# A rational FFN behind masked attention: splitting three blocks of results with one cast and one subtraction, one wide place for the parts and four places for V

## Chip, cores and metric

The kernel runs on one core of one Trainium2 chip. The metric is the time of one launch on the device, in microseconds (us), as the median of several runs. The names used below are PE for TensorE (matmul; PEld is its weight load), DVE for VectorE, ACT for ScalarE, POOL for GpSimd and SP for SyncE.

## The reference

Attention over 8 batches of 8 heads with 576 positions and 64 columns each keeps only scores within `tau` of a row's maximum. Its output, 4608 rows of 512 columns, goes through a feed-forward layer whose activation is a ratio of two polynomials:

```python
scores = scale * np.matmul(q, k.transpose(0, 1, 3, 2))
thresh = np.max(scores, axis=-1, keepdims=True) - tau
scores = np.where(scores >= thresh, scores, -1000000000.0)
attn = np.exp(scores - np.max(scores, axis=-1, keepdims=True))
attn = attn / (np.sum(attn, axis=-1, keepdims=True) + 1e-09)
attn_out = np.matmul(attn, v)
x = attn_out.transpose(0, 2, 1, 3).reshape(B * S, H * D)
h = x @ w_in                      # 512 -> 2048
P = a[0] + a[1] * h + a[2] * h**2 + a[3] * h**3
Q = 1.0 + np.abs(b[0]) * np.abs(h) + np.abs(b[1]) * h**2
g = P / (Q + 1e-06)
return g @ w_out                  # 2048 -> 512
```

## The kernel before

**Attention.** Heads go in pairs; a batch has four pairs. A unit is one tile of 128 query rows of a pair, or the remainder of 64 rows. PE computes the scores of both heads (L812 and L816, the remainder L805) into banks of PSUM. DVE takes the negated maxima (L822), ACT applies the threshold (L837) and the exponential with its sum (L841). DVE and ACT scale the result and split it into a high and a low half of 16 bits (L326 or L328, then L863). A transposing DMA on SP's queue brings both into `pT`, and PE multiplies them with V, which is split in the same way (L934), into a chunk `x` of 256 rows for the second part. In the first batch the transposition is done by PE (L886, L891) and the product in 32 bits (L917).

**V's places.** V of a pair is loaded (L691) into one of `NV` places. A place comes free when the last product of its pair is done. The scale of a batch's V is found from the maxima of all four pairs (L431 is PE's step in it), so the first product of a batch needs all four to be loaded. The loads stand on POOL's queue from the third batch on, with those of Q and K.

**Feed-forward.** A group is four blocks of 128 of the 2048 columns, for one chunk of 256 rows; there are 72 groups, and the last one is done as two halves. The first product (L1051) is 48 matmuls. ACT brings it to SBUF with a scale (L1060), 1024 columns wide. Then come: the absolute value (L1065 on ACT or L1067 on DVE), two steps of the polynomials on DVE (L1071, L1074), a third (L1084), logarithm and exponential on ACT (L1078, L1081) for the reciprocal, and three more steps on DVE (L1087, L1090, L1093), the last of which gives the results `r`. The first of a group's four blocks goes into the second product as it is, in 32 bits (L1114). The other three are split in parts: a cast (`f_gh`, on ACT at L318 or on DVE at L320) rounds a block of 256 columns to the format `fp32r`, and a subtraction on DVE (`f_gl`, L1101) leaves what the rounding lost. PE multiplies the parts with the two parts of the weights, three matmuls for each block and half of the rows (L1110). The parts of one block lie in a place `g`, of which there are two; a place is free when the six matmuls that read it are done.

**Who sets the order.** Nothing is ordered by hand. The class `Plan` knows a duration for each operation, what it waits for and which places it takes and gives back. It lays out all operations in time on all engines, and the instructions are then written in that order. Operations in the table `FLEX` may go to ACT or DVE; the planner picks one by weighing the two with the factors `START`, `EARLY` and `PRICE`, each in its own stretch of time (`sooner`). Where PE would be idle near the start, it is given filler matmuls (L1254). A place of a pool is taken by the operation that comes next in its line. So a change of a duration or of a pool moves instructions on every engine.

Of the kernel before, what the change touches and what calls it, by code (L numbers as in the profile page):

```python
# [8 lines left out]
F32 = mybir.dt.float32  # L9
F32R = mybir.dt.float32r  # L10
F16 = mybir.dt.float16
# [4 lines left out]
ALU = mybir.AluOpType  # L16
# [7 lines left out]

POOLS = {"e": 3, "hi": 2, "pT": 2, "st": 8, "sc": 2, "t": 8, "u": 3, "g": 2, "x": 3, "xr": 1}

B2, B3, BA, B1, BH = [(0, 1, 2), (3, 4, 5)], [(0, 1, 2)], [(3,), (4,), (5,)], [(7,), (6,), (5,)], [(5,), (6,)]


LEAD, SPACE0, SPACING = 4.776489494, 2.7365, 2.085146464
ENDK, ENDS = 4.7452, 10.130284218

WHEN = [(-4.7413, 1.6268), (5.5534, 0.8332), (13.0267, 0.2709), (15.0744, 0.5122)]

V0, V1 = -3.870384768, -4.680004432

SINGLE = 21

VISITED = 8

FIRST = [(0, 0, 8), (1, 0, 16), (0, 8, 16)]
LAST = (0, 1, 2)
SOON = 1

NQ = 2

NV = 5

EARLY_BP = 8

# [4 lines left out]
PARTS = 3  # L57
# [2 lines left out]

ALL = 2.0 ** 100

PLAIN = (0, 1, 2, 3, 4)

UP = 2.0 ** -14
TPD = 1.3
# [11 lines left out]
        "ev": {"ACT": 0.465, "DVE": 0.6}, "ev1": {"ACT": 0.156, "DVE": 0.196}, "A": {"ACT": 0.583, "DVE": 0.341},  # L78
        "gh": {"ACT": 0.31, "DVE": 0.2}, "wh": {"ACT": 0.57, "DVE": 0.38}, "vc": {"ACT": 0.7, "DVE": 0.25}, "twice": {"ACT": 0.2, "DVE": 0.13}}

START = {"ACT": 2.958800008, "DVE": 3.4788}
START_END = 61.53014116
EARLY = {"ACT": 2.0183, "DVE": 2.9268}
EARLY_END = 1205.239479456
PRICE = {"ACT": 0.7389, "DVE": 2.6699}

TOL = {"PE": 0.098890645, "ACT": 0.1137, "DVE": 0.0398, "POOL": 0.1, "DMA": 0, "GD": 0}
WARM, WARM_END = 0.6, 400.0

LOADS_END = 120.0  # L90

LATE = 2.0

SPARE = {'t': 2, 'u': 1, 'g': 1, 'sc': 1}

# [24 lines left out]
class Plan:  # L120
# [21 lines left out]
    def op(self, eng, dur, key, fn, after=(), take=(), drop=()):  # L142
        engs = {eng: dur} if isinstance(eng, str) else eng
        o = Op(engs, key, fn, [x for x in after if x is not None], list(take), list(drop))
        o.rank, o.tiling = self.rank, "ff"
        self.ops.append(o)
        return o
# [10 lines left out]
    def sooner(self, e, t, o, free, can):  # L158
        price = START if t < START_END else EARLY if t < EARLY_END else PRICE
        for x, dur in o.engs.items():  # L160
            if x != e:
                begin = max(free[x], o.ready[x])
                begin += sum(p.engs[x] for p in can[x] if p.key < o.key and len(p.engs) == 1 and p.ready[x] <= begin)
                if begin + dur * price[x] < t + o.engs[e] * price[e]:
                    return True
        return False

    def order(self):
# [6 lines left out]
        free = dict.fromkeys(engines, 0.0)  # L175
        tiling = "f"
# [13 lines left out]
        while left:  # L190
            best = None
            for e in engines:
                starts = []
                for o in can[e]:
                    t = max(free[e], o.ready[e])
                    for h in o.take:
                        spot = None if h.pool in line and line[h.pool][-1] is not h and len(self.pools.get(h.pool, ())) <= SPARE.get(h.pool, 99) else self.spot(h, t)
                        if spot is None:
                            t = None
                            break  # L200
                        t = max(t, spot[0])
                    if t is not None:
                        if e == "PE":
                            t = max(t, free[e] + TURN.get((tiling, o.tiling[0]), 0.0))
                        starts.append((t, o))
                if not starts:
                    continue
                first = min(t for t, _ in starts)
                starts = sorted([x for x in starts if x[0] <= first + TOL[e]] if all(len(o.engs) == 1 for _, o in starts)
                                else starts, key=lambda x: (x[1].key, x[1].n))  # L210

                keep = [(t, o) for t, o in starts if len(o.engs) == 1 or not self.sooner(e, t, o, free, can)]
                if not keep:
                    continue
                first = min(t for t, _ in keep)
                t, o = min(((t, o) for t, o in keep if t <= first + TOL[e]), key=lambda x: (x[1].key, x[1].n))
                if best is None or t < best[0]:
                    best = (t, o, e)
            assert best is not None, "no op can start"
            t, o, e = best  # L220
# [3 lines left out]
            if e == "PE" and self.warm is not None and t < WARM_END:  # L224
                n = int((t - free[e]) * WARM / 0.22)
# [10 lines left out]
            if e == "PE":  # L236
                tiling = o.tiling[1]
# [34 lines left out]
def fr(ap):  # L272
    return ap.bitcast(F32R)
# [3 lines left out]
def masked_attention_rational_ffn(  # L277
# [12 lines left out]
    nc = tc.nc  # L290
    B, NP, D, S = qT.shape
    S = S // 2
    DM, DFF = w_in.shape
    P = 128
    NT = S // P
    REM = S - NT * P
    NF = DFF // P
    NFP = NF // 2
    NC = DM // P
    CT = 256  # L300
# [4 lines left out]
    op = plan.op  # L305
# [10 lines left out]
    def copy(dst, src):  # L316
        if plan.eng == "ACT":
            nc.scalar.copy(dst, src)  # L318
        elif plan.eng == "DVE":
            nc.vector.tensor_copy(dst, src)  # L320
        else:
            nc.gpsimd.tensor_scalar(dst, src, 1.0, 1.0, ALU.mult, ALU.mult)
# [9 lines left out]
    def tensor_tensor(dst, x, y, how):  # L332
# [5 lines left out]

    forms = {"t": ([P, 4 * CT], F32), "u": ([P, DM], F32), "e": ([P, 2 * S], F32), "hi": ([P, 2 * S], F16),
             "pT": ([P, 2, 2, 2 * NT + 1, P], F16), "st": ([P, 8], F32), "sc": ([P, 4], F32),  # L340
             "g": ([P, 2, CT], F32), "x": ([P, 2, NP, CT], F16), "xr": ([P, 2, NP, CT], F16)}
    places = {x: [const.tile(f, d, name=f"{x}{i}") for i in range(POOLS[x])] for x, (f, d) in forms.items()}

    def place(h):
        return places[h.pool][h.slot]
# [181 lines left out]
    for i in range(NW):  # L527
        pieces = []
        for c in range(NC):
            n = i * NC + c  # L530
# [6 lines left out]
            key = w_key(i, c)  # L537

            o6, box = decode_ops(n, key, load, hold)
# [9 lines left out]
        key = w_key(i, NC)  # L549
# [17 lines left out]
    wo_done = []  # L567

    def in_parts(f):
        return f % NC >= NC - PARTS  # L570

    for f in range(NF):
# [6 lines left out]
        key = w_key(f // NC, NC + f % NC)  # L579
# [5 lines left out]
        o, box = decode_ops(NC * NW + f, key, load, hold)  # L585
# [15 lines left out]
    visits = []  # L601
    for bb in range(B):
        v0 = bb * NP
        if bb < VISITED:
            visits += [(v0 + i, half) for i in range(NP - 1)] + [(v0 + NP - 1, half + other + rest)]
            visits += [(v0 + i, other + rest) for i in range(NP - 2, -1, -1)]
        else:
            visits += [(v0 + i, half + other + rest) for i in range(NP)]
# [60 lines left out]

    def is_plain(bp, t):  # L670

        return bp < NP and t in PLAIN

    v_ops = {}

# [343 lines left out]
    def moe_ops(ck, f0, nb, p, begins, ends, soon):  # L1019
# [18 lines left out]
        def on(e, d, *rest):  # L1038
            return op(e, size(e, d), *rest)
# [52 lines left out]
        def f_g():  # L1092
            nc.vector.scalar_tensor_tensor(box["r"], box["r"], a0, box["q"], ALU.add, ALU.mult)  # L1093

        def f_gh(j):
            box["g", j] = place(hg[j])
            copy(fr(box["g", j][:, 0]), box["r"][:, j * CT:(j + 1) * CT])

        def f_gl(j):
            g = box["g", j]  # L1100
            nc.vector.tensor_tensor(fr(g[:, 1]), box["r"][:, j * CT:(j + 1) * CT], g[:, 0], ALU.subtract)  # L1101

        def f_g2(j, tt):
            f = f0 + j
            if begins and j == 0:
                acc[tt] = bank(ah[tt])
            if in_parts(f):
                g = box["g", j][:, :, tt * P:(tt + 1) * P]
                for n, (x, y) in enumerate(((0, 0), (1, 0), (0, 1))):
                    nc.tensor.matmul(acc[tt], fr(g[:, x]), fr(wo[f][y]), start=begins and j == n == 0,  # L1110
                                     stop=ends and j == nb - 1 and n == 2)
                return
            o = j * CT + tt * P
            nc.tensor.matmul(acc[tt], box["r"][:, o:o + P], wo[f], start=begins and j == 0, stop=ends and j == nb - 1)  # L1114
# [30 lines left out]
                                       wi_done[g] + x_done[ck] + wo_done[f0:f0 + nb] + last_g1 if prev is None else [prev],  # L1145
                                       [bhs[j // 2]] if (j % 2, part) == (0, 0) else (), [xo, xo])
        last_g1[:] = [prev]
        hh, hq, hr = Hold("t", 1), Hold("t", 1), Hold("t", 2 * nb)
        n = 1 if kind == "m" else 4
        hs = [b for b in ([bb] if kind == "m" else range(4 * bb, 4 * bb + 4))]  # L1150
        h = None
# [8 lines left out]
        r3 = on("DVE", 0.638, p + 0.67, f_r3, [r2])  # L1160
        ln = on("ACT", 0.632, p + 0.7, f_ln, [q, r3])
        iv = on("ACT", 0.563, p + 0.75, f_inv, [ln])
        e = on("DVE", 0.6075, p + 0.85, f_e, [iv])
        nn = on("DVE", 0.6075, p + 0.9, f_n, [e], (), [hh])
        gd = on("DVE", 0.638, p + 0.95, f_g, [nn, r3], (), [hq])
        hg, gl = {}, {}
        for j in range(nb):
            if in_parts(f0 + j):
                hg[j] = Hold("g", 2)
                o = op(FLEX["gh"], 0, p + 0.97, lambda j=j: f_gh(j), [gd], [hg[j]], [hr])  # L1170
                gl[j] = op("DVE", 0.335, p + 0.98, lambda j=j: f_gl(j), [o], (), [hr])
        if begins:
            accs[ck] = {}, [Hold("acc", 1, BA) for _ in range(2)]
        acc, ah = accs[ck]
# [3 lines left out]
            each.sort(key=lambda x: x[1])  # L1178
        for i, (j, tt) in enumerate(each):
            starts = begins and j == 0  # L1180
            o = op("PE", 0.705 if j in hg else 0.859, p + 1.7 + 0.1 * i, lambda j=j, tt=tt: f_g2(j, tt),
                   [gl.get(j, gd), wo_done[f0 + j], prev, None if starts else last_g2.get(tt)],
                   [ah[tt]] if starts else (), [hg.get(j, hr)])
            prev = last_g2[tt] = o
        if ends:
            prev = None
# [42 lines left out]
    for bb in range(1, B - 1):  # L1229
        order += [(("m", bb, c), range(0, NF, NC)) for c in range(2)]  # L1230
        if bb % 4 == 3:
            order.append((("r", bb // 4, 0), range(0, NF, NC)))
    p = 0.0
    for ck, fs in order:
        kind, bb, c = ck
# [61 lines left out]
```

## Time and profile before

| what | value |
|---|---|
| median of three runs | 1279.27 us (1278.4 to 1280.01) |
| time of the profiled execution | 1281.68 us |
| span of the profiled execution, first to last instruction | 1279.9 us |
| mean granted clock of TensorE | 0.994 |
| busy: PE, DVE, ACT, POOL | 1246.4, 1199.3, 1074.5, 231.3 us |
| first product, L1051, 3072 records with chunks `x` | 374.7 us |
| split second product, L1110, 1296 | 355.2 us |
| subtractions, L1101, 216 on DVE | 86.6 us |
| casts of results, 123 on ACT and 93 on DVE | 47.8 and 25.7 us |

A busy time is the time in which at least one instruction of the group ran; the mean of one is its own duration. On a full engine the durations of neighbours overlap, so the pitch from one to the next is shorter than the mean. A 32-bit matmul of the program (not of `fp32r`) leaves two records. In the tables by stretches of time, the columns are the stretch, its length, the busy time of PE, PEld, DVE, ACT and POOL with the number of instructions, then the granted clock, the share of the DMA engines and GB/s; where one line of the code is asked for, only the engine in question stands there. In the waits, the columns are the engine with what it was to do, what it waited for, the total in us, the number of times and the longest. In the groups, busy time and mean in ns are followed by the idle time just ahead of them and what ended it.

### The profile page before, as it was taken

The page shows a single profiled execution, that of the slowest core. Times are in us where ns is not written, and L with a number is a line of the kernel's source. Part 1 is how long each engine was busy: PE and PEld are TensorE (multiplying, and loading weights), DVE is VectorE, ACT ScalarE, POOL GpSimd, SP SyncE. Part 2 cuts the span into 40 slices and gives each one's busy share as a digit, 9 for nine tenths or more (in the row PEclk, how much of TensorE's full clock was granted, in tenths as well). Part 3 has the DMA queues.
Part 4 walks back from the last instruction along what each step waited for, and adds up shares of the span by engine and source line. Part 5 has one row for each costly group of instructions (what it writes and reads, how often), then busy time and mean ns, then how long its engine had stood idle before and what let it go on. Part 6 is the DMA issues. An engine that isn't in the chain of part 4 may idle for free.

```text
span 1279.9 us, 25127 instructions
## 1 busy us (share of the span) xinstructions
PE 1246.4 (97%) x9252; PEld 889.8 (70%) x9252; DVE 1199.3 (94%) x1960; ACT 1074.5 (84%) x2180; POOL 231.3 (18%) x480
## 2 busy tenths in 40 slices
PE   8899999999999999999999999999999999999998
PEld 6576676676767667766667667677776667677775
DVE  5899999999999999999999899999999999997876
ACT  5999888989999888888897699999988998874454
POOL 2112000132132311332022140322121221100000
PEclk9999999999999999999999999999999999999999
DMA  7645246688667656776442765876566665530000
GB/s 216 174 143 163 78 105 112 134 144 154 105 133 132 146 107 119 142 137 126 91 105 56 131 141 111 142 135 136 104 120 125 130 123 112 111 71 17 18 17 17
DMA packets 338251, 146.64 MB, mean 115 GB/s; under 512 B 314416, under 2 KB 320720, under 8 KB 338128
## 3 DMA queue, kind: packets, MB, share of 16 engines
q1 hardware_dynamic: 316528, 87.67, 38.5%
q0 software_dynamic: 21280, 56.78, 16.4%
q8 instruction: 73, 1.20, 0.4%
q10 hardware_dynamic: 320, 0.59, 0.2%
q14 instruction: 50, 0.41, 0.1%
HBM read 60.30 MB, written 9.44 MB: 54 GB/s over the span
## 4 chain that ended last, share of the span: by engine, by line
PE 53%; DVE 27%; ACT 8%; issue 5%; DMA 3%; SPq 0%; DVEq 0%; ACTq 0%
PE banks L1051 16%; PE banks L1110 15%; PE banks L1114 6%; PE banks L934 6%; PE banks L816 5%; DVE e L863 4%; DVE st L822 3%; DMA pT<-e 2%; DVE t L1071 2%; DVE t L1087 2%; DVE t L1090 2%; PE banks L805 2%; DVE t L1084 2%; DVE t L1093 2%; DVE g L1101 2%
## 5 line engine op out<-in xcount | busy, mean ns | idle before, releaser
L1051 PEld LDWEIGHTS <-wi 128*128 128x128 f16 x3456 | 324.1, 98 | 144.1 <-issue 108.0
L1051 PE MATMUL banks<-x,wi 128*128 128x256 f16 x3072 | 374.7, 275 | 3.0 <-ACT t L1060 1.7
L1110 PE MATMUL banks<-wp,g 128*128 128x512 f32 x1296 | 355.2, 415 | 1.9 <-ACT g L318 1.2
L1110 PEld LDWEIGHTS banks<-wp,g 128*128 128x128 f32 x1296 | 234.0, 189 | 70.9 <-issue 15.5
L837 ACT ACTIVATE e<-banks,st 128x576 f32<-128x576 f32 x288 | 206.4, 735 | 18.5 <-DVE st L831 11.1
L841 ACT ACTIVATE e<-e,cf 128x576 f32<-128x576 f32 x288 | 221.0, 774 | 0.3
L863 DVE SCALAR_TENSOR_TENSOR e<-e,st,hi 128x576 f16<-128x576 f32 x252 | 203.5, 808 | 3.9 <-ACT hi L326 3.4
L822 DVE TENSOR_REDUCE st<-banks 128x2 f32<-128x1152 f32 x128 | 171.8, 1342 | 12.9 <-PE banks L816 10.8
L326 ACT ACTIVATE hi<-e,st 128x576 f16<-128x576 f32 x177 | 134.0, 769 | 51.9 <-DVE st L852 41.1
L816 PE MATMUL banks<-KK,QQ 64*128 64x512 f32 x512 | 144.5, 641 | 0.0
L1114 PE MATMUL banks<-wp,t 128*128 128x512 f32 x288 | 142.2, 608 | 1.7 <-DVE t L1093 1.6
L1060 ACT ACTIVATE t<-banks,hsc 128x512 f32<-128x512 f32 (+1 forms) x192 | 106.3, 575 | 25.9 <-PE banks L1051 24.7
L934 PEld LDWEIGHTS <-V 128*64 128x64 f16 x2520 | 104.1, 111 | 33.8 <-issue 32.6
L934 PE MATMUL banks<-pT,V 128*64 128x256 f16 (+1 forms) x2520 | 118.9, 249 | 3.0 <-DMA pT<-e 3.0
L1087 DVE SCALAR_TENSOR_TENSOR t<-t,co,t 128x1024 f32<-128x1024 f32 (+1 forms) x73 | 92.0, 1261 | 22.7 <-ACT t L1081 22.7
L1078 ACT ACTIVATE t<-t,co 128x1024 f32<-128x1024 f32 (+1 forms) x73 | 82.7, 1133 | 12.8 <-DVE t L1084 12.7
L1093 DVE SCALAR_TENSOR_TENSOR t<-t,co,t 128x1024 f32<-128x1024 f32 (+1 forms) x73 | 92.0, 1261 | 0.5
L1071 DVE SCALAR_TENSOR_TENSOR t<-t,co 128x1024 f32<-128x1024 f32 (+1 forms) x73 | 92.0, 1260 | 0.0
L1084 DVE SCALAR_TENSOR_TENSOR t<-t,co,t 128x1024 f32<-128x1024 f32 (+1 forms) x73 | 91.9, 1260 | 0.0
L1074 DVE SCALAR_TENSOR_TENSOR t<-t,co 128x1024 f32<-128x1024 f32 (+1 forms) x73 | 91.9, 1259 | 0.0
L1101 DVE TENSOR_TENSOR g<-t,g 128x256 fp32r<-128x256 f32 x216 | 86.6, 414 | 2.0 <-ACT g L318 1.6
L1090 DVE SCALAR_TENSOR_TENSOR t<-t,t 128x1024 f32<-128x1024 f32 (+1 forms) x73 | 87.7, 1201 | 0.4
(137 smaller groups left out, 1518.2 us busy)
## 6 DMA issues: line engine op xcount, KB each, us to landing
KK<-in_kT_dram POOLq DMA_DIRECT2D x84, 144.0 KB, 3.9
t<-in_w_in_dram POOLq DMA_DIRECT2D x16, 512.0 KB, 5.8
t<-in_w_out_dram POOLq DMA_DIRECT2D x16, 512.0 KB, 4.7
V<-in_v_dram POOLq DMA_DIRECT2D x24, 256.0 KB, 4.4
out_dram<-u POOLq DMA_DIRECT2D x24, 256.0 KB, 2.7
QQ<-in_qT_dram POOLq DMA_DIRECT2D x42, 144.0 KB, 3.1
QQ<-in_qT_dram POOLq DMA_DIRECT2D x42, 128.0 KB, 3.4
KK<-in_kT_dram SPq DMA_DIRECT2D x24, 144.0 KB, 3.5
```

The costliest lines, as they stand in the source:

```text
L326: nc.scalar.activation(dst, src, AF.Identity, scale=factor)
L816: nc.tensor.matmul(d, QQ[r, t * P:(t + 1) * P], KK[r, REM:S], **one)
L822: nc.vector.tensor_reduce(box["st"][:, 0:2], box["both"], AX.X, ALU.max, negate=True)
L837: nc.scalar.activation(ev(hh), box["s"][hh], AF.Prelu, scale=SCALE, bias=box["st"][:, 2 + hh:3 + hh], alpha=STEEP)
L841: nc.scalar.activation(e, e, AF.Exp, scale=passes, accum_out=box["st"][:, 4 + hh:5 + hh])
L863: nc.vector.scalar_tensor_tensor(box["lo"][:, c], ev(hh), box["st"][:, 6 + hh:7 + hh], box["hi"][:, c], ALU.mult, ALU.subtract)
L934: nc.tensor.matmul(dst, V[:, c * P + head * D:c * P + (head + 1) * D], rhs, start=c == 0 and n == 0, stop=c == NT and n == 2)
L1051: nc.tensor.matmul(d, wi_tile(c, f0 + j, hl), x[:, c, :], start=c == 0 and n == 0, stop=c == NC - 1 and n == 2)
L1071: nc.vector.scalar_tensor_tensor(box["r"], box["h"], a2, box["h"], ALU.add, ALU.mult)
L1087: nc.vector.scalar_tensor_tensor(box["q"], box["q"], qc, box["i"], ALU.add, ALU.mult)
L1110: nc.tensor.matmul(acc[tt], fr(g[:, x]), fr(wo[f][y]), start=begins and j == n == 0, stop=ends and j == nb - 1 and n == 2)
L1114: nc.tensor.matmul(acc[tt], box["r"][:, o:o + P], wo[f], start=begins and j == 0, stop=ends and j == nb - 1)
```

## The change

The cast and the subtraction of a group's blocks in parts become one instruction each, over the columns of all these blocks: 768 for a whole group, 256 and 512 for the two halves of the last one. Their place `g` is three times as wide, and there is one instead of two. V has four places instead of five. The planner's durations for the two operations follow, the planner looks at places when it weighs an engine (`sooner`), and a number of its factors have other values. Names that are new beside these (`REST_FIRST`, `STICK`, the form of `PLAIN`, the last lines on `LAST`) have values with which they change nothing by themselves.

```diff
-POOLS = {"e": 3, "hi": 2, "pT": 2, "st": 8, "sc": 2, "t": 8, "u": 3, "g": 2, "x": 3, "xr": 1}
+POOLS = {"e": 3, "hi": 2, "pT": 2, "st": 8, "sc": 2, "t": 8, "u": 3, "g": 1, "x": 3, "xr": 1}
...
-LEAD, SPACE0, SPACING = 4.776489494, 2.7365, 2.085146464
-ENDK, ENDS = 4.7452, 10.130284218
+LEAD, SPACE0, SPACING = 4.46212747, 2.7365, 2.085146464
+ENDK, ENDS = 4.7452, 7.461352888
...
-NV = 5
+NV = 4
...
-EARLY_END = 1205.239479456
-PRICE = {"ACT": 0.7389, "DVE": 2.6699}
+EARLY_END = 1196.621762778
+PRICE = {"ACT": 0.779887252, "DVE": 2.581335568}
...
-                begin = max(free[x], o.ready[x])
+                begin = max([free[x], o.ready[x]] + [self.spot(h, 0.0)[0] for h in o.take])
...
-             "g": ([P, 2, CT], F32), "x": ([P, 2, NP, CT], F16), "xr": ([P, 2, NP, CT], F16)}
+             "g": ([P, 2, PARTS * CT], F32), "x": ([P, 2, NP, CT], F16), "xr": ([P, 2, NP, CT], F16)}
...
-        def f_gh(j):
-            box["g", j] = place(hg[j])
-            copy(fr(box["g", j][:, 0]), box["r"][:, j * CT:(j + 1) * CT])
-
-        def f_gl(j):
-            g = box["g", j]
-            nc.vector.tensor_tensor(fr(g[:, 1]), box["r"][:, j * CT:(j + 1) * CT], g[:, 0], ALU.subtract)
+        split = [j for j in range(nb) if in_parts(f0 + j)]
+        GW = len(split) * CT
+
+        def f_gh():
+            box["g"] = place(hg)[:, :, 0:GW]
+            copy(fr(box["g"][:, 0]), box["r"][:, split[0] * CT:split[0] * CT + GW])
+
+        def f_gl():
+            g = box["g"]
+            nc.vector.tensor_tensor(fr(g[:, 1]), box["r"][:, split[0] * CT:split[0] * CT + GW], g[:, 0], ALU.subtract)
...
-                g = box["g", j][:, :, tt * P:(tt + 1) * P]
+                o = (j - split[0]) * CT + tt * P
+                g = box["g"][:, :, o:o + P]
...
-        hh, hq, hr = Hold("t", 1), Hold("t", 1), Hold("t", 2 * nb)
+        hh, hq, hr = Hold("t", 1), Hold("t", 1), Hold("t", 2 * (nb - len(split) + 1))
...
-        hg, gl = {}, {}
-        for j in range(nb):
-            if in_parts(f0 + j):
-                hg[j] = Hold("g", 2)
-                o = op(FLEX["gh"], 0, p + 0.97, lambda j=j: f_gh(j), [gd], [hg[j]], [hr])
-                gl[j] = op("DVE", 0.335, p + 0.98, lambda j=j: f_gl(j), [o], (), [hr])
+        n = len(split)
+        hg = Hold("g", 2 * n)
+        gh = {e: d * n + (n - 1) * -{"ACT": 0.098, "DVE": 0.07}[e] for e, d in FLEX["gh"].items() if e == "DVE" or not soon}
+        gh = op(gh, 0, p + 0.97, f_gh, [gd], [hg], [hr])
+        gl = op("DVE", 0.068 + 0.2667 * n, p + 0.98, f_gl, [gh], (), [hr])
```

Three places show how the instructions move. The first is DVE in the middle of the program, at the split of the 26th group: `t5_73` holds its results, `g0_96` and `g1_97` are the two places, `e0_79`, `st0_86` and `hi1_83` belong to the softmax and `V2_163` is a place of V. Before:

```order
L1101 TENSOR_TENSOR g1_97<-t5_73,g1_97 128x256
L863 SCALAR_TENSOR_TENSOR e0_79<-e0_79,st0_86,hi1_83 128x576
L950 SCALAR_TENSOR_TENSOR xr0_101<-banks_67,xr0_101 128x64
L863 SCALAR_TENSOR_TENSOR e0_79<-e0_79,st0_86,hi1_83 128x576
L1101 TENSOR_TENSOR g0_96<-t5_73,g0_96 128x256
L750 SCALAR_TENSOR_TENSOR V2_163<-V2_163,sx_166,u0_76 128x640
L320 CAST g1_97<-t5_73 128x256
L320 COPY V2_163<-u0_76 128x640
L1101 TENSOR_TENSOR g1_97<-t5_73,g1_97 128x256
```

The same engine at the split of the 26th group after the change (`t2_70` holds the results; L1101 is now the last step of the polynomials and L1112 the subtraction):

```order
L1101 SCALAR_TENSOR_TENSOR t2_70<-t2_70,co_126,t4_72 128x1024
L325 CAST g0_96<-t2_70 128x768
L1075 TENSOR_SCALAR t5_73<-t7_75 128x1024
L1112 TENSOR_TENSOR g0_96<-t2_70,g0_96 128x768
L1079 SCALAR_TENSOR_TENSOR t1_69<-t7_75,co_126 128x1024
L1082 SCALAR_TENSOR_TENSOR t5_73<-t5_73,co_126 128x1024
```

The cast and subtraction of the group stand together right behind its results, instead of three pairs spread among the softmax's instructions. Over the whole program DVE has 216 subtractions before and 73 after, 93 casts before and 35 after; ACT has 123 casts before and 38 after.

The second place is PE at the end of the program, where the last whole group ends (`wp11` is its last block's weights) and the two halves follow (blocks 12 and 13, then 14 and 15). Before:

```order
L1110 MATMUL banks_67<-wp11_1_153,g0_96 128x512
L1114 MATMUL banks_67<-wp12_154,t3_71 128x512 x2
L1110 MATMUL banks_67<-wp13_0_155,g1_97 128x512 x2
L1110 MATMUL banks_67<-wp13_1_156,g1_97 128x512
L1110 MATMUL banks_67<-wp13_0_155,g1_97 128x512 x2
L1110 MATMUL banks_67<-wp13_1_156,g1_97 128x512
L1110 MATMUL banks_67<-wp14_0_157,g0_96 128x512 x2
L1110 MATMUL banks_67<-wp14_1_158,g0_96 128x512
L1110 MATMUL banks_67<-wp15_0_159,g1_97 128x512 x2
```

After:

```order
L1122 MATMUL banks_67<-wp11_1_152,g0_96 128x512
L1126 MATMUL banks_67<-wp12_153,t2_70 128x512 x2
L1122 MATMUL banks_67<-wp13_0_154,g0_96 128x512 x2
L1122 MATMUL banks_67<-wp13_1_155,g0_96 128x512
L1122 MATMUL banks_67<-wp13_0_154,g0_96 128x512 x2
L1122 MATMUL banks_67<-wp13_1_155,g0_96 128x512
L1122 MATMUL banks_67<-wp14_0_156,g0_96 128x512 x2
L1122 MATMUL banks_67<-wp14_1_157,g0_96 128x512
L1122 MATMUL banks_67<-wp15_0_158,g0_96 128x512 x2
```

The matmuls are the same in the same order, but blocks 13 and 14, which were in two places, now follow each other in one.

The third place is POOL's queue in the middle of the program, where the fourth V of a batch is loaded between loads of Q and K. Before:

```order
L654 DMA KK0_115<-in_kT_dram 64x576
L655 DMA KK0_115<-in_kT_dram 64x576
L691 DMA V4_165<-in_v_dram 128x4x128
L695 DMA V4_165<-in_v_dram 64x64 x2
L719 MEMSET V4_165 64x64 x2
```

After:

```order
L662 DMA KK0_114<-in_kT_dram 64x576
L663 DMA KK0_114<-in_kT_dram 64x576
L699 DMA V3_163<-in_v_dram 128x4x128
L703 DMA V3_163<-in_v_dram 64x64 x2
L727 MEMSET V3_163 64x64 x2
```

The load stands where it stood among the others, but goes to one of four places instead of one of five.

More of the change, by code (lines that the diff above doesn't have):

```diff
@@ L23 @@
 TINY = 2.0 ** -60
-POOLS = {"e": 3, "hi": 2, "pT": 2, "st": 8, "sc": 2, "t": 8, "u": 3, "g": 2, "x": 3, "xr": 1}
+POOLS = {"e": 3, "hi": 2, "pT": 2, "st": 8, "sc": 2, "t": 8, "u": 3, "g": 1, "x": 3, "xr": 1}
 B2, B3, BA, B1, BH = [(0, 1, 2), (3, 4, 5)], [(0, 1, 2)], [(3,), (4,), (5,)], [(7,), (6,), (5,)], [(5,), (6,)]
-LEAD, SPACE0, SPACING = 4.776489494, 2.7365, 2.085146464
-ENDK, ENDS = 4.7452, 10.130284218
-WHEN = [(-4.7413, 1.6268), (5.5534, 0.8332), (13.0267, 0.2709), (15.0744, 0.5122)]
-V0, V1 = -3.870384768, -4.680004432
+LEAD, SPACE0, SPACING = 4.46212747, 2.7365, 2.085146464
+ENDK, ENDS = 4.7452, 7.461352888
+WHEN = [(-4.7413, 1.6268), (5.5534, 0.8332), (13.0267, 0.2709), (17.317172867, 0.340859863)]
+V0, V1 = -4.053118584, -4.680004432
 SINGLE = 21
@@ L44 @@
 LAST = (0, 1, 2)
+REST_FIRST = ()
 SOON = 1
 NQ = 2
-NV = 5
+NV = 4
 EARLY_BP = 8
@@ L61 @@
 ALL = 2.0 ** 100
-PLAIN = (0, 1, 2, 3, 4)
+PLAIN = {0: (0, 1, 2, 3, 4), 1: (0, 1, 2, 3, 4), 2: (0, 1, 2, 3, 4), 3: (0, 1, 2, 3, 4)}
 UP = 2.0 ** -14
@@ L79 @@
         "gh": {"ACT": 0.31, "DVE": 0.2}, "wh": {"ACT": 0.57, "DVE": 0.38}, "vc": {"ACT": 0.7, "DVE": 0.25}, "twice": {"ACT": 0.2, "DVE": 0.13}}
-START = {"ACT": 2.958800008, "DVE": 3.4788}
+START = {"ACT": 3.34080024, "DVE": 3.4788}
 START_END = 61.53014116
 EARLY = {"ACT": 2.0183, "DVE": 2.9268}
-EARLY_END = 1205.239479456
-PRICE = {"ACT": 0.7389, "DVE": 2.6699}
-TOL = {"PE": 0.098890645, "ACT": 0.1137, "DVE": 0.0398, "POOL": 0.1, "DMA": 0, "GD": 0}
+EARLY_END = 1196.621762778
+PRICE = {"ACT": 0.779887252, "DVE": 2.581335568}
+TOL = {"PE": 0.098890645, "ACT": 0.1137, "DVE": 0.025166682, "POOL": 0.1, "DMA": 0, "GD": 0}
 WARM, WARM_END = 0.6, 400.0
@@ L92 @@
 LATE = 2.0
+STICK = 0.0
 SPARE = {'t': 2, 'u': 1, 'g': 1, 'sc': 1}
@@ L215, in order @@
                 first = min(t for t, _ in keep)
-                t, o = min(((t, o) for t, o in keep if t <= first + TOL[e]), key=lambda x: (x[1].key, x[1].n))
+                near = [x for x in keep if x[0] <= first + TOL[e]]
+                t, o = min(near, key=lambda x: (x[1].key + (STICK if e == "PE" and x[1].tiling[0] != tiling else 0.0), x[1].n))
                 if best is None or t < best[0]:
@@ L603, in masked_attention_rational_ffn @@
         v0 = bb * NP
-        if bb < VISITED:
+        if bb in REST_FIRST:
+            visits += [(v0 + i, half + rest) for i in range(NP - 1)] + [(v0 + NP - 1, half + rest + other)]
+            visits += [(v0 + i, other) for i in range(NP - 2, -1, -1)]
+        elif bb < VISITED:
             visits += [(v0 + i, half) for i in range(NP - 1)] + [(v0 + NP - 1, half + other + rest)]
@@ L670, in is_plain @@
     def is_plain(bp, t):
-        return bp < NP and t in PLAIN
+        return t in PLAIN.get(bp, ())
     v_ops = {}
@@ L1162, in moe_ops @@
         iv = on("ACT", 0.563, p + 0.75, f_inv, [ln])
-        e = on("DVE", 0.6075, p + 0.85, f_e, [iv])
+        e = on("DVE", 0.638, p + 0.85, f_e, [iv])
         nn = on("DVE", 0.6075, p + 0.9, f_n, [e], (), [hh])
         gd = on("DVE", 0.638, p + 0.95, f_g, [nn, r3], (), [hq])
-        hg, gl = {}, {}
-        for j in range(nb):
-            if in_parts(f0 + j):
-                hg[j] = Hold("g", 2)
-                o = op(FLEX["gh"], 0, p + 0.97, lambda j=j: f_gh(j), [gd], [hg[j]], [hr])
-                gl[j] = op("DVE", 0.335, p + 0.98, lambda j=j: f_gl(j), [o], (), [hr])
+        n = len(split)
[3 more added lines that the diff above has]
+        gl = op("DVE", 0.068 + 0.2667 * n, p + 0.98, f_gl, [gh], (), [hr])
         if begins:
@@ L1180, in moe_ops @@
             starts = begins and j == 0
-            o = op("PE", 0.705 if j in hg else 0.859, p + 1.7 + 0.1 * i, lambda j=j, tt=tt: f_g2(j, tt),
-                   [gl.get(j, gd), wo_done[f0 + j], prev, None if starts else last_g2.get(tt)],
-                   [ah[tt]] if starts else (), [hg.get(j, hr)])
+            o = op("PE", 0.705 if j in split else 0.859, p + 1.7 + 0.1 * i, lambda j=j, tt=tt: f_g2(j, tt),
+                   [gl if j in split else gd, wo_done[f0 + j], prev, None if starts else last_g2.get(tt)],
+                   [ah[tt]] if starts else (), [hg if j in split else hr])
             prev = last_g2[tt] = o
@@ L1232, in masked_attention_rational_ffn @@
             order.append((("r", bb // 4, 0), range(0, NF, NC)))
+    order += [(x, range(0, NF, NC)) for i, x in enumerate((("m", B - 1, 0), ("m", B - 1, 1), ("r", B // 4 - 1, 0))) if i not in LAST]
     p = 0.0
```

## The prediction

> **What bounds the kernel now.** I read the page's head and its chain first, then the table of windows by stage, then what TensorE (PE) waited for, and last single stretches of time. The page:
>
> ```profile
> span 1279.9 us, 25127 instructions
> ...
> PE 1246.4 (97%) x9252; PEld 889.8 (70%) x9252; DVE 1199.3 (94%) x1960; ACT 1074.5 (84%) x2180; POOL 231.3 (18%) x480
> ...
> PE 53%; DVE 27%; ACT 8%; issue 5%; DMA 3%; SPq 0%; DVEq 0%; ACTq 0%
> ```
>
> PE and DVE (VectorE) are both nearly full, and the chain runs through DVE for 27% of the span. The change takes work from DVE, so the question is how much of PE's time is really waiting. By stage (columns: length, then busy time of each engine):
>
> ```profile
> 0.00:192.00 192.00, 176.30 (x1293) 129.82 (x1294) 168.00 (x386) 166.73 (x357) 30.10 (x77) 0.98 0.52 147
> 192.00:1152.00 960.00, 948.23 (x7245) 669.22 (x7244) 933.17 (x1456) 848.01 (x1718) 201.24 (x403) 1.00 0.63 121
> 1152.00:1216.00 64.00, 64.00 (x394) 48.76 (x393) 51.27 (x61) 26.68 (x39) 0.00 (x0) 1.00 0.05 17
> ```
>
> In the middle PE is idle for 960 - 948.23 = 11.8 us and in the first stage for 15.7; in the tail's first half, where attention is over, not at all, with DVE at 51.27 of 64. A busy PE could still be a slow one, so I look at two stretches of the tail, the first from the timeline, the second from the chain in order of time (start, length):
>
> ```profile
> 1166.72 4.76 PE L1051 MATMUL banks<-x,wi 128*128 128x256 f16 x42
> ```
> ```profile
> 1171.48 1.72 PE banks L1114 x4
> ```
>
> The next piece starts at 1171.32 in that timeline, so a first-product matmul takes 4.60 / 42 = 0.110 us when nothing is in its way. The line L1051 in the two stages:
>
> ```profile
> 192.00:1152.00 960.00, 332.59 (x2722) 1.00 0.63 121
> 1152.00:1216.00 64.00, 30.27 (x262) 1.00 0.05 17
> ```
>
> That is 0.122 us each in the middle against 0.116 in the tail: PE is dense there as well, and the rest is mostly its turns between kinds of matmul. So PE's work is the floor, and only its waits can be won. Waits of PE in the middle (total, times, longest), and two of them in the timeline:
>
> ```profile
> PE banks L812 <- ACT e L837: 3.8, 4, 1.2
> PE banks L934 <- DMA pT<-e: 3.0, 2, 2.3
> PE banks L1051 <- ACT t L1060: 1.7, 2, 1.4
> PE banks L1110 <- ACT g L318: 1.2, 1, 1.2
> PE banks L1051 <- DVE xr L950: 1.2, 2, 0.9
> PE banks L1114 <- DVE t L1093: 0.4, 1, 0.4
> PE banks L1110 <- DVE g L1101: 0.4, 1, 0.4
> ```
> ```profile
> 606.77 1.97 PE L934 MATMUL banks<-pT,V 128*64 128x256 f16 x28 [2.32 <-DMA pT<-e]
> ...
> 751.29 5.76 PE L1051 MATMUL banks<-x,wi 128*128 128x256 f16 x36 [1.35 <-ACT t L1060]
> ```
>
> They are few and have many causes. The granted clock (after PE's busy time and those of the other engines) falls behind each of the two:
>
> ```profile
> 606.00:610.00 4.00, 3.23 (x35) 2.47 (x35) 2.70 (x4) 1.62 (x5) 0.00 (x0) 0.76 0.19 40
> 610.00:614.00 4.00, 4.00 (x32) 3.30 (x31) 4.00 (x5) 4.00 (x8) 0.00 (x0) 0.81 0.54 104
> ...
> 750.00:754.00 4.00, 2.71 (x14) 1.97 (x14) 4.00 (x9) 4.00 (x9) 3.73 (x7) 0.68 0.81 187
> 754.00:758.00 4.00, 4.00 (x30) 2.90 (x28) 3.02 (x6) 4.00 (x9) 0.34 (x1) 0.89 0.78 164
> ```
>
> The lost clock is worth 4 x (0.24 + 0.19) = 1.7 us and 4 x (0.32 + 0.11) = 1.7 us. The whole pot of the middle is 11.8 + 3.4 = 15.2 us.
>
> **The subtraction and the cast.** The rows of both, and of their only wider relatives, the weights' split:
>
> ```profile
> L1101 DVE TENSOR_TENSOR g<-t,g 128x256 fp32r<-128x256 f32 x216 | 86.6, 414 | 2.0 <-ACT g L318 1.6
> L592 DVE TENSOR_TENSOR wp<-t,wp 128x512 fp32r<-128x512 f32 x12 | 8.2, 683 | 0.1
> L320 DVE CAST g<-t 128x256 fp32r<-128x256 f32 x93 | 25.7, 285 | 2.2 <-PE banks L1110 1.5
> L320 DVE CAST wp<-t 128x512 fp32r<-128x512 f32 x8 | 3.5, 436 | 0.0
> L318 ACT CAST g<-t 128x256 fp32r<-128x256 f32 x123 | 47.8, 401 | 41.9 <-PE banks L1110 35.7 <-DVE t L1093 5.3
> L318 ACT CAST wp<-t 128x512 fp32r<-128x512 f32 x4 | 2.8, 688 | 0.3 <-DVE t L333 0.2
> ```
>
> The durations overlap where the engine is full; what one costs in the queue is its pitch, from the chain in order of time:
>
> ```profile
> 442.47 0.41 DVE g L320 x2
> 442.88 0.67 DVE g L1101 x2
> ```
>
> So a narrow subtraction costs 0.335 us and a narrow cast 0.205. Each further 256 columns cost 683 - 414 = 269 ns and 436 - 285 = 151 ns. A wide subtraction is 0.335 + 2 x 0.269 = 0.873, a wide cast 0.205 + 2 x 0.151 = 0.507. Subtractions: 216 x 0.335 = 72.4 before; 71 x 0.873 and 0.335 + 0.604 for the two short ones make 62.9 after. Casts on DVE: 93 before, 19.1 us; 34 wide ones and one of 512 columns after, 17.6 us. DVE saves 9.5 + 1.5 = 11.0 us, which is far less than three instructions for one suggests: the columns remain, only 143 + 58 starts go. ACT has 123 casts before and 37 wide and one narrow after. With 688 - 401 = 287 ns for each further 256 columns, one is 0.401 + 0.574 = 0.975 us, and ACT goes from 47.8 to 36.5. ACT is not the floor; I count nothing for it.
>
> **What the new order moves.** The planner also deals the other flexible operations anew: 22 instructions come to DVE and 34 leave it (the leaving ones are mostly short copies, the coming ones include five searches for a maximum over 512 columns and five scalings of 576). At the mean of a DVE instruction, 1199.3 / 1960 = 0.61 us, twelve fewer would be 7 us; as the long ones come, I count zero. The filler matmuls of the start fall from 82 to 80, so the start waits as before: 0, between -4 and +4 (a quarter of its 15.7 us of idle). The number of other PE instructions is the same.
>
> **How much of the 11 us reaches the end.** The lower bound is the chain's share: 11.0 x 27% = 3 us. The upper bound is the pot, 15.2. I take the waits that the changed operations or DVE itself end, 1.2 + 1.2 + 0.4 + 0.4 = 3.2 us, and one of the two clock dips, 1.7 (the one at 751, 40 us behind the g waits): 4.9 us. That is near the lower end, because the larger waits end with ACT or a transpose's DMA. The Trainium skill, TensorE: Matmul & The Clock Gate, section "Why this matters for your kernels", says that throughput drops need idle gaps of over about 3 us; by it the dip would not belong to these waits and the gain would be 3.2. Here gaps of 2.32, and of 0.86 and 1.35 close together, already have a dip behind them, so the measurement decides.
>
> **One place for the parts.** Before, a cast could go to the second place while PE read the first. Now it waits until the last of 18 matmuls has read the place, and the subtraction and PE's next matmuls wait behind it; on ACT the softmax queues behind a waiting cast. The handover, from the end of the span before the change:
>
> ```profile
> 1266.68 0.42 DVE L1101 TENSOR_TENSOR g<-t,g 128x256 fp32r<-128x256 f32 x1
> ...
> 1267.15 1.43 PE L1110 MATMUL banks<-wp,g 128*128 128x512 f32 x5 [0.30 <-DVE g L1101]
> ...
> 1268.54 1.98 PE L1114 MATMUL banks<-wp,t 128*128 128x512 f32 x4
> 1268.57 0.41 ACT L318 CAST g<-t 128x256 fp32r<-128x256 f32 x1 [0.39 <-PE banks L1110]
> 1269.06 0.42 DVE L1101 TENSOR_TENSOR g<-t,g 128x256 fp32r<-128x256 f32 x1
> ```
>
> PE to ACT 0.03, cast to subtraction 0.08, subtraction to PE 0.05; with a wide cast of 0.975 and a wide subtraction of 0.952 (0.414 + 0.538) that is 2.1 us. Against it stands what PE has to do between two groups' split matmuls in the new order. Counted in that order with the pace of its own rows, it is 5.0 us or more at all 61 handovers ahead of the tail, so nothing there. In the tail it is 2.4 us at three places (two plain second products, 1.72, and six first products, 0.66), 1.7 at the last full group and nothing between the two half groups, where a cast of 512 columns and its subtraction, 0.44 + 0.68, stand bare, as 0.30 and 0.9 us of PE's waits did before. I add +0.5 (0 to +4: one DVE instruction of 1.2 us in the way at three of them).
>
> **Sum.** Start 0, middle -4.9, tail +0.5: -4.4 us. The profiled execution took 1281.68 us with a span of 1279.9, so its own time becomes 1277.3; the median of the runs shown is 1279.27, 2.41 us lower, and the same step from it gives 1274.9.
>
> **Rivals.** First, DVE is the bound and PE merely looks full. The Trainium skill, Trainium Kernel Development and Optimization, section "Best Practices", calls matmul busy time a bad measure of distance to the roofline and names weight loads instead, which are at 70% here. Then all 11 us would come, and the time would be 1268.5. The 0.110 us pace speaks against it, DVE's 933 of 960 in the middle for it: chance 0.12. Second, no change: the waits that go come back with other causes, because the order is new everywhere and nothing in the row of waits is tied to g alone. Time 1279, chance 0.28. Third, slower, by the places of V. With four of them the next batch's last V load waits for the old batch's last product with V:
>
> ```profile
> POOL V L691 <- PE banks L934: 155.9, 16, 18.9
> ...
> V<-in_v_dram POOLq DMA_DIRECT2D x24, 256.0 KB, 4.4
> ```
>
> The load lands 4.4 us behind its issue; then come the maximum, the scale and the split of V, all on busy engines. In the new order three score units lie between the old batch's last product and the new one's first at the later boundaries. There are 128 whole and 32 remainder units in 1280 us, 8 us each, so 24 us stand against the 4.4 and five short steps, by my estimate some 15 us with the queues they wait in. It decides once the sequence takes over 24 us: with 1.5 us of idle and 1.7 of clock at six boundaries minus the 4.4 it would be 19 - 4.4, a time of 1284 to 1294. Chance 0.18.
>
> **Chances.** My forecast has 0.42, most of it faster. A change of 0.2%, 2.6 us, is about what the measurement can tell. Faster 0.12 + 0.40 = 0.52, same 0.29, slower 0.19. The range goes from just under the first rival, 1267, to 1284, where the third begins; the forecast's own is 1271 to 1278.
>
> **What would show it.** Right: 71 subtractions of about 0.95 us, DVE's busy time 10 to 20 us lower, PE's unchanged within 4, PE's idle in the middle at about 8 us with no wait on g. Wrong: PE waits on g in the middle (the single place), PE waiting on V or its scale at a boundary, or new waits on L837 and transposes that fill the pot again.

## The result, and the profile after

The changed kernel takes 1273.12 us as the median of five runs (1270.45 to 1274.86), the kernel before 1279.73 us beside it (1278.4 to 1280.58). The ratio is 0.995, with a 95% interval from 0.9934 to 0.9965: faster by 6.6 us, where the forecast was 4.4. The gain is small, and the interval reaches from 4.5 to 8.4 us. Differences to the changed kernel below are differences of such medians, and about 2 us of doubt are in each of them.

The page of the profiled execution, which at 1270.45 us is the fastest of the five (that of the kernel before was 1281.68, so the two profiles lie 11.2 us apart and not 6.6):

```profile
span 1268.7 us, 24824 instructions
...
PE 1238.4 (98%) x9248; PEld 890.3 (70%) x9248; DVE 1188.2 (94%) x1747; ACT 1063.8 (84%) x2104; POOL 231.8 (18%) x480
```

DVE's busy time falls by 11.1 us. The table by stages (length, then busy time of PE, PEld, DVE, ACT and POOL, then the granted clock):

```profile
0.00:192.00 192.00, 172.19 (x1300) 126.41 (x1302) 167.04 (x375) 169.60 (x356) 26.39 (x72) 0.99 0.54 151
192.00:1152.00 960.00, 955.13 (x7297) 679.51 (x7294) 936.54 (x1289) 842.79 (x1666) 205.40 (x408) 1.00 0.62 121
1152.00:1216.00 64.00, 64.00 (x395) 49.57 (x393) 45.64 (x44) 22.88 (x31) 0.00 (x0) 1.00 0.03 9
1216.00:1269.00 53.00, 47.10 (x265) 34.78 (x263) 38.95 (x42) 28.49 (x53) 0.00 (x0) 0.99 0.07 21
```

and the end of the kernel before:

```profile
1216.00:1280.00 64.00, 57.86 (x326) 42.05 (x324) 46.84 (x60) 33.07 (x68) 0.00 (x0) 0.98 0.06 17
```

PE's idle time in the middle falls from 11.8 us to 4.9, in the start it rises from 15.7 to 19.8, and at the end it is 5.6 (1268.7 - 1216 - 47.10) after 6.0 (1279.9 - 1216 - 57.86). That is 3 us together. The other 8 us between the profiles are PE's busy time, 1246.4 before and 1238.4 after, for the same matmuls. The mean granted clock, 0.994 before and 0.998 in this execution, is worth some 5 us of it by an estimate (0.004 of the span). What is left, 3 us, is not pinned to a row.

What PE still waits for in the middle:

```profile
PE banks L820 <- ACT e L845: 2.9, 2, 2.2
PE banks L1122 <- DVE g L1112: 1.2, 2, 0.8
PE banks L942 <- DMA pT<-e: 0.3, 1, 0.3
PE banks L942 <- DVE V L325: 0.2, 1, 0.2
```

The seven rows of before have become four. The waits on a transpose (3.0 us), on the first product's way to SBUF (L1060, 1.7), on `xr` (1.2) and on the last step of the polynomials (0.4) are gone or nearly so. The waits on `g`, 1.6 us in two rows before, are 1.2 us with the one wide place. The groups of the wide instructions:

```profile
L1112 DVE TENSOR_TENSOR g<-t,g 128x768 fp32r<-128x768 f32 x71 | 67.3, 947 | 0.2
L323 ACT CAST g<-t 128x768 fp32r<-128x768 f32 x37 | 30.6, 826 | 9.4 <-DVE t L1101 6.7 <-PE banks L1122 2.6
L325 DVE CAST g<-t 128x768 fp32r<-128x768 f32 x34 | 18.7, 551 | 3.4 <-PE banks L1122 2.9
```

### The profile page after: what moved, and what is told of

Same layout as the page of the kernel before. It is cut to its first block, busy times and chain, and to the rows that moved or that the text cites. A ratio compares the mean times of both kernels' runs of the same rounds, so it can differ in the third digit from the quotient of the medians.

```text
span 1268.7 us, 24824 instructions
## 1 busy us (share of the span) xinstructions
PE 1238.4 (98%) x9248; PEld 890.3 (70%) x9248; DVE 1188.2 (94%) x1747; ACT 1063.8 (84%) x2104; POOL 231.8 (18%) x480
## 5 line engine op out<-in xcount | busy, mean ns | idle before, releaser
L1059 PE MATMUL banks<-x,wi 128*128 128x256 f16 x3072 | 367.3, 273 | 2.9 <-ACT pT L323 1.5
L1122 PE MATMUL banks<-wp,g 128*128 128x512 f32 x1296 | 343.4, 411 | 2.0 <-DVE g L1112 1.5
L1122 PEld LDWEIGHTS banks<-wp,g 128*128 128x128 f32 x1296 | 236.0, 188 | 68.3 <-issue 11.2
L331 ACT ACTIVATE hi<-e,st 128x576 f16<-128x576 f32 x172 | 130.8, 770 | 49.9 <-DVE st L860 47.6
L1101 DVE SCALAR_TENSOR_TENSOR t<-t,co,t 128x1024 f32<-128x1024 f32 (+1 forms) x73 | 91.9, 1259 | 0.4
L655 POOL DMA_DIRECT2D QQ<-in_qT_dram x42 | 22.2, 528 | 335.4 <-PE banks L813 180.6
```

Source lines behind the costliest of these rows:

```text
L331: nc.scalar.activation(dst, src, AF.Identity, scale=factor)
L1059: nc.tensor.matmul(d, wi_tile(c, f0 + j, hl), x[:, c, :], start=c == 0 and n == 0, stop=c == NC - 1 and n == 2)
```

## Experiments

The first theory was that the saved starts on DVE and ACT bring the gain. Its rival was that the new order and the planner's new numbers bring it. A third, the prediction's own reading, was that PE is the floor and DVE's time counts for a part only.

**Undoing the merge in the same order.** The operations stay where the planner put them; only what each of them writes is cut in pieces.

```diff
-            copy(fr(box["g"][:, 0]), box["r"][:, split[0] * CT:split[0] * CT + GW])
+            for i in range(len(split)):
+                o = (split[0] + i) * CT
+                copy(fr(box["g"][:, 0, i * CT:(i + 1) * CT]), box["r"][:, o:o + CT])
...
-            nc.vector.tensor_tensor(fr(g[:, 1]), box["r"][:, split[0] * CT:split[0] * CT + GW], g[:, 0], ALU.subtract)
+            for i in range(len(split)):
+                o, c = (split[0] + i) * CT, slice(i * CT, (i + 1) * CT)
+                nc.vector.tensor_tensor(fr(g[:, 1, c]), box["r"][:, o:o + CT], g[:, 0, c], ALU.subtract)
```

> The changed kernel in its own order, places and planner's numbers, but each wide cast and each wide subtraction is written as three (two, one) narrow ones in the same spot. DVE's queue then has 142 more subtractions' starts and 69 more casts' starts, about 11 us by the pitches. Theory 1, the saved starts on DVE and ACT bring the gain: most of the 6.6 us goes, 1277 to 1281 us. Theory 2, the new order and the planner's numbers bring it, and the merging itself is off PE's path: 1272 to 1275 us.

Measured: 1281.88 us, ratio to the kernel before 1.0018 (1.0009 to 1.0028), that is 8.8 us above the changed kernel and just above the range of the first theory. So in its own order the merging is worth 8.8 us, more than the whole gain, and what is left of the change (order, places, numbers) costs 2.3 us (1281.88 against the 1279.63 of the kernel before on that chip). The price on DVE is more than the 11 us that were expected. This order leaves 104 narrow casts to DVE where the old order left 93, so the pitches of the prediction give 104 x 0.205 - 17.6 = 3.7 us for the casts and 9.5 for the subtractions, 13.2 together; DVE's busy time is 13.6 us longer (1201.8 and 1188.2). As PE's order is the same in both kernels, the last product with V, a row of PE's timeline, shows where the time was lost. First the changed kernel, then the narrow one:

```profile
1147.62 2.30 PE L942 MATMUL banks<-pT,V 128*64 128x256 f16 x60
```
```profile
1159.27 2.30 PE L942 MATMUL banks<-pT,V 128*64 128x256 f16 x60
```

The whole 11.5 us by which these two spans differ (1280.2 and 1268.7) are there before the tail begins; the tail is as long in both, 121 us. The starts of the 128 whole score units, read from the same timeline, show it creeping in: 0.4 us at the 25th unit, 1.5 at the 37th, 3.4 at the 77th, 7.2 at the 81st, and 11.7 at the last. The step of 3.8 us is one place. The 80th unit waits 3.79 us there for its bank, against 2.25 in the changed kernel, and the clock behind the wait is 0.50, where the profile of the changed kernel has 1.00:

```profile
714.14 0.80 PE L820 MATMUL banks<-KK,QQ 128*128 128x128 f32 x2 [3.79 <-ACT e L845]
```
```profile
716.00:720.00 4.00, 4.00 (x13) 1.76 (x10) 2.98 (x7) 2.94 (x6) 0.00 (x0) 0.50 0.00 0
```

In both profiles DVE has stood at this place for the transposing DMA of `hi` (3.50 us here, 4.15 in the changed kernel); here ACT then stands 1.69 us for that of `e` as well. Whether the merging spares that second wait, or the one execution of the changed kernel escaped it, is not shown.

**One half of it each.** The same edit for the subtraction alone and for the cast alone.

> The changed kernel in its own order with the wide casts, but each wide subtraction written as three narrow ones in the same spot: 9.5 us more on DVE by the pitches, nothing more on ACT. Theory 1, DVE's time in the middle reaches the end nearly in full: 1279 to 1282 us, that is most of the 8.8 us that narrow casts and subtractions together cost. Theory 2, the price was ACT's casts (37 x 3 instead of 37) or the starts themselves: 1273 to 1276 us.

Measured: 1279.47 us, ratio 1.0005 (0.9995 to 1.0014), 6.4 us above the changed kernel for 9.5 us of DVE by the pitches, which is two thirds.

> The changed kernel in its own order with the wide subtractions, but each wide cast written as three narrow ones in the same spot: 1.5 us more on DVE, some 7 us more on ACT. Theory 1: 1273 to 1276 us. Theory 2: 1277 to 1282 us.

Measured: 1275.51 us, ratio 0.9973 (0.9964 to 0.9982), 2.4 us above the changed kernel, little more than the doubt. The two sum to 8.8 us, what both together cost; that they do so exactly is chance. The subtraction is the larger part, and the first theory holds for DVE. For ACT it is not shown: the narrow casts lengthen DVE's work by 3.7 us in this order and not by the 1.5 expected, and two thirds of 3.7 are 2.5 us, so the 6.0 us more of ACT's busy time (1069.8 and 1063.8) need not have cost anything.

**More work for PE.** A first-product matmul is repeated, two in a group:

```diff
                 for n, (hl, x) in enumerate(((0, xh), (0, xl), (1, xh))):
+                    if c == 0 and n == 0 and j % 2 == 0:
+                        nc.tensor.matmul(d, wi_tile(c, f0 + j, hl), x[:, c, :], start=True, stop=True)
```

> The changed kernel in its own order, with one first-product matmul repeated at the start of each pair of blocks (144 more, 0.11 us each, 15.8 us of PE's time; the values stay). Theory 1, strong form, DVE sets the pace of the middle and PE only follows: the 120 of them ahead of the tail are hidden and the time rises by 3 to 7 us, to 1276 to 1280. Theory 3, PE is the floor everywhere, as the prediction has it: all of it comes, 1287 to 1290 us. Between: both are on the path.

Measured: 1284.66 us, ratio 1.0054 (1.0035 to 1.0073), 11.5 us above the changed kernel for 15.8 us of PE. Most of it comes in the middle, as the last product with V shows:

```profile
1160.89 2.30 PE L942 MATMUL banks<-pT,V 128*64 128x256 f16 x60
```

It is 13.3 us later, for 13.2 us of matmuls (120 x 0.11) ahead of it. The profiled execution of the changed kernel lies 2.7 us below its median, so the profiles show somewhat more than the medians do. PE's time counts in the middle too, and the strong form of the first theory falls.

**More work for ACT, less for DVE.** In `f_gh` the cast is always `nc.scalar.copy`, at the spot where it stood.

> The changed kernel in its own order, but the 35 casts that the planner gave to DVE go to ACT at the same spot: 17.6 us less on DVE, some 29 us more on ACT (0.83 each). Theory 1: DVE's time counts and ACT has room, 1262 to 1270 us. Rival: ACT is as much on the path as DVE (its casts hold up the softmax behind them, and PE waits most often for ACT), 1273 to 1285 us.

Measured: 1280.32 us, ratio 1.0009 (0.9998 to 1.002), 7.2 us above the changed kernel. The rival holds. The new waits are named in the list of all engines:

```profile
ACT g L1108 <- PE banks L1122: 17.4, 5, 5.8
DVE g L1112 <- ACT g L1108: 15.6, 14, 3.0
```

ACT, which has 16% of the span free, stands in line for the one place, with the softmax behind it, and DVE stands in line for ACT.

**Less work for DVE, less work for PE.** The subtraction covers two of the three blocks (the third's low part stays zero), or PE leaves out the product of the high part with the weights' low part. The fill with zeros and the moved `stop` of the matmuls are not shown in these excerpts:

```diff
-            nc.vector.tensor_tensor(fr(g[:, 1]), box["r"][:, split[0] * CT:split[0] * CT + GW], g[:, 0], ALU.subtract)
+            n = min(GW, 2 * CT)
+            nc.vector.tensor_tensor(fr(g[:, 1, 0:n]), box["r"][:, split[0] * CT:split[0] * CT + n], g[:, 0, 0:n], ALU.subtract)
```
```diff
-                for n, (x, y) in enumerate(((0, 0), (1, 0), (0, 1))):
+                for n, (x, y) in enumerate(((0, 0), (1, 0))):
```

> The changed kernel in its own order, with the wide subtraction over two of the three blocks only (the third block's low part stays zero, so its correction is left out): 71 x 0.27 = 19 us less on DVE. Theory 1, DVE's time counts at two thirds in this direction too: 1259 to 1264 us. Rival, the floor of PE is near and the gain of a further saving is small: 1267 to 1272 us.

Measured: 1272.09 us, ratio 0.9946 (0.9926 to 0.9966). Against the changed kernel's 0.995 that is no difference that can be told: 19 us less on DVE by the pitches (15.2 of busy time, 1172.9 and 1188.2) bring 1.0 us, give or take 3. The first theory expected 9 to 14. The two profiles show that a little did come and went again at one place. At the 79th score unit this kernel is 2.1 us ahead of the changed one; the 80th then waits 4.60 us instead of 2.25, again with a clock of 0.50 behind it, and at the last unit the kernel is 1.4 us behind. What the other engines stand for there is the transposing DMA, first DVE and then, for 2.13 us, ACT:

```profile
703.10 0.52 DVE L333 TENSOR_SCALAR hi<-e,st 128x576 f16<-128x576 f32 x1 [4.27 <-DMA pT<-hi]
```
```profile
709.38 0.80 PE L821 MATMUL banks<-KK,QQ 128*128 128x128 f32 x2 [4.60 <-ACT e L846]
```

So outside this place less work on DVE is worth some 2.5 us of 19 in these two executions, and PE is busy for 954.22 of the middle's 960 us.

> The changed kernel in its own order, without the third of the three matmuls of the split second product (high part with the weights' low part is left out): 432 of 0.24 us, 104 us less on PE. If PE is the floor with DVE close behind, the tail (72 of them, 17 us) comes nearly in full and of the 86 us of the middle only what DVE and ACT leave, some 10 to 30: 1225 to 1250 us. If PE alone were the floor: 1170 to 1190 us.

Measured: 1259.35 us, ratio 0.9848 (0.9825 to 0.987): 13.8 us of the 104 come, less than expected. In the profiles the last product with V is 8.7 us earlier (1138.88 and 1147.62), and the tail is 6.0 us shorter. In the middle the table by stages and PE's waits read now:

```profile
192.00:1152.00 960.00, 900.67 (x6985) 616.72 (x6982) 942.74 (x1297) 842.15 (x1668) 204.87 (x408) 1.00 0.62 121
```
```profile
PE banks L820 <- ACT e L845: 36.2, 44, 2.3
PE banks L1126 <- DVE t L1101: 9.0, 12, 1.5
```

PE waits 44 times for a score bank and 12 times for the polynomials, and DVE is busy for 942.74 of 960 us. So the middle has a second floor close below PE's. That it is DVE is read from its busy time and not shown by a run: the score banks wait for ACT's exponential, casts added to ACT cost time above, and no run takes work from PE and DVE together. Adding to PE or to DVE costs two thirds to three quarters of what was added, and taking from one alone brings little.

**Plannings that were not fitted.** Here the planner lays everything out anew. The first takes the changed kernel with the old numbers, the second the kernel before with the new ones, the third the kernel before with `NV = 4`, the last two move `LEAD` alone. With `LEAD` at 4.80 the planner of the kernel before reaches a point where no operation can start, so that step has no time.

> The changed kernel (wide instructions, one wide place, four places for V), planned with the numbers of the kernel before (LEAD, ENDS, WHEN, V0, START, EARLY_END, PRICE, TOL, without the look at places in sooner, the old duration of one step). Theory 1: the gain stays, 1271 to 1275 us. Theory 2, the new numbers bring it: 1278 us or more.

Measured: 1292.14 us, ratio 1.01 (1.0084 to 1.0117), in the second range.

> The kernel before (narrow instructions, two narrow places, five places for V), planned with the new numbers and the look at places. Theory 1: no gain, 1278 to 1284 us. Theory 2: 1271 to 1275 us.

Measured: 1291.61 us, ratio 1.01 (1.0082 to 1.0118), above both ranges.

> The kernel before with four places for V instead of five and nothing else changed; the planner makes a new order. If the fifth place was worth something (the third rival of the prediction), the time rises by 3 us or more, with waits of PE at the batch boundaries; if it was worth nothing, 1277 to 1283 us, the spread that a new order alone brings.

Measured: 1299.69 us, ratio 1.016 (1.014 to 1.018). The waits of PE at the batch boundaries, which would have marked V's places as the cause, are hardly there: in its middle PE waits 0.5 us for V.

> The changed kernel with LEAD 4.48 instead of 4.46212747; nothing else. As for the kernel before: 1279 to 1294 us if any order that was not fitted costs 6 to 20 us, 1271 to 1277 us if the order matters little.

Measured: 1291.05 us, ratio 1.0091 (1.0071 to 1.0112), 18 us above the changed kernel for a change of 0.4% in one number.

> The kernel before with LEAD 4.74 instead of 4.776489494 and nothing else: another order of the same instructions. If any order that was not fitted costs some 12 to 20 us, as it does for the changed kernel, 1290 to 1300 us; then the 20 us of the kernel with four places for V say nothing on V. If the order of the kernel before is not special, 1277 to 1283 us; then they belong to V's places.

Measured: 1282.81 us, ratio 1.0043 (1.0026 to 1.006): 5.3 us above the 1277.54 of the kernel before on that chip, for a change of 0.8%. That lies in the second range of what was expected, at its upper end.

All five are slower than the kernel from which they come, by 5 to 20 us. Each set of numbers is good for its own kernel only, so from these runs neither the numbers nor the structure can be credited alone. Whether the 20 us of the third are the price of V's fifth place or of an order that nobody fitted is not settled: the last run puts the price of another order of that kernel at 5 us, which speaks for V's places; the run before it puts it at 18 for the changed kernel, and PE hardly waits for V, which speaks against them.

## Why the prediction was right, and where it was off

- **DVE's saving** was put at 11.0 us; DVE's busy time fell by 11.1. In that sum the new order takes back some of what the merging saves, 13.6 us in one order. The wide subtraction was put at 0.952 us and measures 0.947. The wide cast on ACT was put at 0.975 and measures 0.826: the four weights' casts at the start were no good measure of its further columns.
- **How much of it reaches the end** is the step that was mis-sized: 4.9 us were taken, between 3 and 15.2, and 8.8 came in the kernel's own order, two thirds of DVE's 13.2. The step counted only waits of PE that the profile puts down to the changed operations or to DVE, and one fall of the clock. But of the 11.5 us between the profiles of the narrow and the changed kernel only 4.9 are idle time of PE (1280.2 - 1245.0 = 35.2 and 1268.7 - 1238.4 = 30.3). The other 6.6 are PE's busy time, 1245.0 and 1238.4, for the same matmuls in the same order. Some 2 us of it, by an estimate, are the slow clock behind the 80th unit (4 us at 0.50); where the rest lies is not pinned to rows. It fits this that waits on ACT and on transposes were in part DVE's lateness, passed on; no run follows a single wait. The share of DVE in the chain, 27%, was a lower bound and no estimate.
- **The sum** came within 2.2 us in part by luck: this step was 3.9 us too small a gain, and the start, the tail and the new order, +0.5 in the sum, cost 2.3.
- **PE is the floor**: half right. More PE work comes at 11.5 of 15.8 us, but 104 us less bring 13.8. PE was the first floor, and a second one lay close below it.
- **The start** was put at 0, between -4 and +4; PE's idle time there rose by 4.1 us. **One place for the parts** was put at no wait in the middle and +0.5 us in the tail. In the middle PE waits 1.2 us for `g`, after 1.6 before; at the end it is idle for 0.4 us less. Order, places and start together cost the 2.3 us of the narrow kernel, which the sum had at +0.5.
- **The first rival**, DVE as the bound and 1268.5 us (1279.27 - 11.0 is 1268.3), missed by 4.6 us. It had the wrong floor, since with 19 us less on DVE the time stays nearly where it is, but it was right that DVE's time counts beyond the waits put down to it. The section "Best Practices" of the Trainium skill's Trainium Kernel Development and Optimization calls matmul busy time a bad measure of the distance to the roofline. The runs agree to this extent: from a PE that is 98% busy, 78 us of busy time could be taken (1160.0 with a matmul of three left out), and the time fell by 13.8 us alone.
- **The second rival**, that the waits come back elsewhere, did not happen: PE's idle time in the middle went from 11.8 to 4.9 us. **The third**, V's four places, did not either: PE waits 0.2 us for V in the middle.
- **The signs** that the prediction set were met by DVE's rows, 71 wide subtractions of 0.947 us and 11.1 us less of busy time. Not met were PE's busy time, which was to stay within 4 us and fell by 8.0, and its idle time in the middle, 4.9 and not 8. A wait on `g`, 1.2 us, is left, where none was expected.

## What to carry to other kernels

Where two engines are full to within a few per cent in an order that is laid out ahead, what is cut from one is worth much of its time (two thirds here) up to the distance to the other, and little beyond; an extra in the same order (a narrow form, a repeated matmul) measures which side one is on better than busy shares do. Merging instructions saves their starts and not their columns, so its worth is the pitch of the narrow ones less that of the wide one, read from a full queue. And a tuned planner is part of the kernel: a comparison that plans anew measures the fit of its numbers, which was 5 to 20 us here, up to three times the effect in question.

## What was not expected of the hardware

The granted clock falls behind some gaps of PE and not behind others of the same length. In the kernel before a gap of 2.32 us had a clock of 0.76 and 0.81 behind it. In the changed kernel a gap of 2.25 us has none:

```profile
709.10 0.49 PE L820 MATMUL banks<-KK,QQ 128*128 128x128 f32 x2 [2.25 <-ACT e L845]
```
```profile
708.00:712.00 4.00, 2.90 (x14) 1.60 (x15) 4.00 (x5) 4.00 (x9) 0.00 (x0) 1.00 0.82 159
712.00:716.00 4.00, 3.61 (x40) 2.17 (x39) 4.00 (x9) 2.73 (x7) 0.00 (x0) 1.00 0.16 29
```

In the run with more work for PE the same score unit waits as long, and the clock behind it falls to 0.60:

```profile
716.34 0.49 PE L820 MATMUL banks<-KK,QQ 128*128 128x128 f32 x2 [2.25 <-ACT e L845]
```
```profile
716.00:720.00 4.00, 3.66 (x12) 1.72 (x13) 3.40 (x5) 3.55 (x8) 0.00 (x0) 0.60 1.05 110
```

The five runs of the changed kernel fit that: mean clocks of 0.999, 0.998, 0.996, 0.996 and 0.995 go with 1271.6, 1270.5, 1273.1, 1274.0 and 1274.9 us. The four runs with `LEAD` at 4.48 do not: the highest clock, 1.000, belongs to the slowest, 1292.2 us. So a part of the spread between runs of one kernel, 4 us here, may be which gap meets a fall of the clock. The Trainium skill, TensorE: Matmul & The Clock Gate, section "Part 1: The HAM clock gate (the 'warmup' mystery)", calls the window in which activity is watched free-running, so that a kernel meets it at a phase that differs from run to run. That the phase at a later gap differs as well is drawn from it here; the runs agree with that, though none of them shows the window itself.
